# RWKV-6 attention, Fourier mixing and an MLP on one core: twelve chunks instead of six transposed by DMA, and a new written-out order

## The chip, the cores and the metric

The kernel runs on 1 core of one Trainium2 chip. The metric is device microseconds of one launch, and lower is better. In short below: PE is TensorE, DVE is VectorE, ACT is ScalarE, POOL is GpSimd, SP is SyncE.

## The reference, cut to what matters

Batch 4, 8 heads, 768 time steps, head dimension 48, all in fp32. First a recurrent attention:

```python
for t in range(S):
    cur = einsum('bhd,bhe->bhde', u * k[t], v[t])
    y[t] = einsum('bhd,bhde->bhe', r[t], state + cur)
    state = w[t][..., None] * state + einsum('bhd,bhe->bhde', k[t], v[t])
```

Its result is laid out as x of (4, 768, 384) and goes through a mixing layer:

```python
u = x + real(fft(fft(x, axis=1), axis=2))
un = (u - mean(u)) / sqrt(var(u) + 1e-6)
out = u + maximum(un @ w_ch1, 0) @ w_ch2      # 384 -> 1536 -> 384
```

## The kernel before

**Attention.** A batch is cut into 6 chunks of 128 time steps, so there are 24 chunks, numbered n = 6b + c; "chunk 2.3" is chunk 3 of batch 2. `attention(b, c)` (line 923) takes one chunk: ACT takes the logarithm of w (`lb`), PE sums it along the chunk with two triangular matrices (lines 939 and 943), ACT takes the exponentials (lines 945 and 958), and the result scales r (line 977, on DVE, in `rkh`) and k (through the helper at line 532, on POOL or DVE, in the other half of `rkh`). Both are then turned, so that the head dimension lies on the partitions: `rkh` (time by head and dimension) becomes `rkt`. From `rkt` PE forms the scores (line 1009, 8 matmuls), DVE masks them (line 1014), and PE forms the output from the masked scores and v (line 1059) and from the carried state (line 1056). The six chunks of batch 0 are done in pairs by `attention2`, with work of the same kind.

**The turning** is done in one of two ways, chosen by `n >= DMA_T`. Below it, PE transposes r and k in 4 matmuls each (lines 993 and 999) into two PSUM banks, and ACT or DVE copies each bank to `rkt` (lines 555 and 556, a tile of 128x512). From it on, one transposing DMA on SP's queue (line 985) turns both at once, from SBUF to SBUF. `DMA_T` is 18: the six chunks of batch 3 go by DMA, those of batches 1 and 2 by PE. The activations of the MLP (`un`, line 1169 on PE, line 1175 as a DMA) are turned the same two ways; with `DMA_U = 2`, batches 2 and 3 go by DMA.

**Mixing and MLP.** `mix(b)` takes the Fourier transforms as matmuls with tables (lines 1123 and 1146), normalizes, and runs the MLP on two halves of 384 rows: 72 matmuls of 128x384 with w_ch1 (line 1193), the ReLU on ACT or DVE (lines 1200 and 1198), 72 with w_ch2 (line 1211), the last sum on DVE (line 1215) and a store (line 1219).

**Data.** The inputs come in as 128x8x48 pieces of 192 KB, one DMA for each of w, k, r and v of a chunk (line 592; batch 0 in pairs, line 584). All loads, stores and transposing DMAs but the two for the MLP's weights stand in one queue, SP's, and SP takes them one after another: where it waits for data to transpose, the loads behind it wait too. Each input has 7 buffers; `rkh` and `rkt` have 4.

**Order.** Nothing is left to run time. The kernel records all its operations, and the table `ORDER` says for each of the five engines in which order it runs them and, where an operation may run on several engines, on which. The table came from a planner, outside the kernel, that works with the lengths in the code (an operation's second argument, and `xfer`, `DMA_SET`, `T_RK` and their like for DMAs). The kernel runs that plan once while it is built (`schedule`), only to give tiles their PSUM banks and to place the waits; the lengths have no effect on the chip beyond that.

Of the kernel before, what the change touches and what calls it, by code (L numbers as in the profile page):

```python
# [22 lines left out]
DMA_T, DMA_U, T_RK, T_UN, T_XFER = 18, 2, 1750, 2000, 1800  # L23
# [35 lines left out]
    "act": (  # L59
# [12 lines left out]
    "dve": (  # L72
# [15 lines left out]
    "pool": (  # L88
# [11 lines left out]
}  # L100


class _Tile:


# [26 lines left out]
class _Prog:  # L132
# [7 lines left out]
    DMA_SET, DMA_POST, DMA_SW = 1400, 300, 2000  # L140
# [1147 lines left out]
```

## Time and profile before

| | us |
|---|---|
| three runs | 184.34, 185.72, 187.69 |
| median | 185.72 |
| the profiled execution, its own time | 186.0 |
| its span, first to last instruction | 184.2 |
| PE busy in the span | 175.2 (95%) |
| DVE, ACT, POOL busy | 155.6, 123.4, 105.0 |
| share of the 16 DMA engines, SP's queue | 63.8% |

The span is divided by the profile in several views: busy time by stretch, the chain of work that ended last (each piece with what released it), groups of instructions by source line, and waits by engine. A matmul's duration there is the time from its start to its modelled end; matmuls overlap, so the pace of a run of them is read from the chain, where only the part that moves the chain on is counted. A DMA's row has the time that SP needed to issue it; "to landing" is from issue to the last byte.

### The profile page before, as it was taken

The page shows a single profiled execution, that of the slowest core. Times are in us where ns is not written, and L with a number is a line of the kernel's source. Part 1 is how long each engine was busy: PE and PEld are TensorE (multiplying, and loading weights), DVE is VectorE, ACT ScalarE, POOL GpSimd, SP SyncE. Part 2 cuts the span into 40 slices and gives each one's busy share as a digit, 9 for nine tenths or more (in the row PEclk, how much of TensorE's full clock was granted, in tenths as well). Part 3 has the DMA queues.
Part 4 walks back from the last instruction along what each step waited for, and adds up shares of the span by engine and source line. Part 5 has one row for each costly group of instructions (what it writes and reads, how often), then busy time and mean ns, then how long its engine had stood idle before and what let it go on. Part 6 is the DMA issues. An engine that isn't in the chain of part 4 may idle for free.

```text
span 184.2 us, 4725 instructions
## 1 busy us (share of the span) xinstructions
PE 175.2 (95%) x1824; PEld 125.8 (68%) x1824; DVE 155.6 (84%) x374; ACT 123.4 (67%) x291; POOL 105.0 (57%) x126
## 2 busy tenths in 40 slices
PE   5989999999999999899997999999999999999993
PEld 2446677776778777577865777668787766887661
DVE  8999999999989999989999789999797497551343
ACT  4898999998999676699986789836514521146010
POOL 2027998699785739999796386994654330000000
PEclk9999999999999999999999999999999999999999
DMA  5999899999999998998989996635601014520033
GB/s 154 320 324 256 189 180 178 182 196 214 149 204 194 184 192 170 210 264 165 194 211 206 204 205 171 117 66 114 191 4 43 4 43 109 130 102 4 0 126 130
DMA packets 102599, 29.00 MB, mean 157 GB/s; under 512 B 98865, under 2 KB 102066, under 8 KB 102450
## 3 DMA queue, kind: packets, MB, share of 16 engines
q1 hardware_dynamic: 102034, 26.36, 63.8%
q0 software_dynamic: 544, 2.36, 7.0%
q8 instruction: 14, 0.23, 0.5%
q14 instruction: 7, 0.06, 0.1%
HBM read 23.59 MB, written 4.72 MB: 154 GB/s over the span
## 4 chain that ended last, share of the span: by engine, by line
PE 53%; DVE 16%; ACT 11%; POOL 6%; SPq 5%; DMA 4%; issue 3%; POOLq 0%; DVEq 0%
PE bank L1211 20%; PE bank L1193 16%; SPq L592 5%; PE bank L1146 4%; ACT rkt L555 2%; PE bank L1123 2%; DMA in_v<-in_v_dram 2%; PE bank L1232 2%; DMA in_w<-in_w_dram 2%; DVE x L1065 2%; DVE rkh L532 2%; POOL rk L532 2%; ACT lb L546 1%; DVE ah L1014 1%; ACT vb L546 1%
## 5 line engine op out<-in xcount | busy, mean ns | idle before, releaser
L1193 PE MATMUL bank<-unt,w 128*128 128x384 bf16 x288 | 55.6, 328 | 0.1
L1211 PE MATMUL bank<-w,ht 128*128 128x384 bf16 (+2 forms) x300 | 54.8, 320 | 0.0
L1200 ACT ACTIVATE ht<-bank 128x384 bf16<-128x384 f32 x72 | 32.9, 497 | 24.5 <-PE bank L1193 24.2
L1193 PEld LDWEIGHTS bank<-unt,w 128*128 128x128 bf16 x288 | 38.8, 144 | 6.2 <-ACT ht L1200 0.4
L1211 PEld LDWEIGHTS bank<-w,ht 128*128 128x128 bf16 x300 | 28.1, 98 | 15.2
L1014 DVE TENSOR_TENSOR ah<-bank,msk 128x512 bf16<-128x512 f32 x36 | 23.1, 680 | 1.0 <-PE bank L1009 1.0
L532 POOL TENSOR_TENSOR rk<-rk,ub 128x384 f32<-128x384 f32 x21 | 21.0, 1006 | 2.8 <-DVE rk L532 2.0
L1215 DVE SCALAR_TENSOR_TENSOR osb<-bank,rstd,uf 128x384 f32<-128x384 f32 (+2 forms) x25 | 14.8, 593 | 6.6 <-ACT rstd L1183 3.8
L532 POOL TENSOR_TENSOR vtd<-in_v,dc 128x384 f32<-128x384 f32 (+1 forms) x23 | 19.1, 834 | 2.2 <-DVE dc L966 1.1
L1198 DVE TENSOR_SCALAR ht<-bank 128x384 bf16<-128x384 f32 x24 | 12.5, 550 | 8.9 <-PE bank L1193 8.9
L555 ACT ACTIVATE rkt<-bank 128x512 bf16<-128x512 bf16 x28 | 17.2, 637 | 1.7 <-PE bank L999 0.7
L532 POOL TENSOR_TENSOR rk<-in_r,in_k 128x384 f32<-128x384 f32 x17 | 17.1, 1014 | 1.9 <-DMA in_k<-in_k_dram 0.9
L532 POOL TENSOR_TENSOR rkh<-in_k,e 128x384 bf16<-128x384 f32 x16 | 15.9, 1004 | 2.9 <-ACT e L958 1.7
L532 POOL TENSOR_TENSOR xf<-sd 128x382 bf16<-128x382 f32 (+1 forms) x12 | 12.0, 1003 | 8.1 <-DVE sd L532 3.1
L532 POOL TENSOR_TENSOR sd<-x 128x385 f32<-128x385 f32 x8 | 8.1, 1007 | 10.7 <-DVE sd L532 8.8
L546 ACT ACTIVATE un<-uf,agg 128x384 bf16<-128x384 f32 x18 | 10.8, 620 | 3.9 <-DVE agg L1154 3.9
L1148 DVE TENSOR_TENSOR uf<-bank,x 128x384 f32<-128x384 f32 x24 | 12.5, 546 | 0.6 <-PE bank L1146 0.5
L1152 DVE BATCH_NORM_STATS2 bst<-uf 128x6 f32<-128x384 f32 x24 | 12.9, 547 | 0.1
L546 ACT ACTIVATE lb<-in_w 128x384 bf16<-128x384 f32 (+1 forms) x21 | 11.8, 572 | 1.5 <-DMA in_w<-in_w_dram 1.4
L546 ACT ACTIVATE vb<-in_v 128x384 bf16<-128x384 f32 x23 | 11.8, 520 | 1.2 <-DMA in_v<-in_v_dram 1.2
L977 DVE TENSOR_TENSOR rkh<-bank,in_r 128x384 bf16<-128x384 f32 x18 | 9.8, 549 | 2.5 <-ACT bank L945 1.5
L945 ACT ACTIVATE bank<-bank 128x384 f32<-128x384 f32 x18 | 8.8, 488 | 3.9 <-PE bank L939 3.9
(163 smaller groups left out, 359.7 us busy)
## 6 DMA issues: line engine op xcount, KB each, us to landing
out_dram<-osb SPq DMA_DIRECT2D x23, 192.0 KB, 2.1
in_w<-in_w_dram SPq DMA_DIRECT2D x18, 192.0 KB, 4.0
in_r<-in_r_dram SPq DMA_DIRECT2D x18, 192.0 KB, 4.4
in_k<-in_k_dram SPq DMA_DIRECT2D x18, 192.0 KB, 4.2
in_v<-in_v_dram SPq DMA_DIRECT2D x18, 192.0 KB, 4.1
w<-in_moe_w_ch_dram POOLq DMA_DIRECT2D x2, 1152.0 KB, 9.6
in_r<-in_r_dram SPq DMA_DIRECT2D x3, 384.0 KB, 4.6
in_k<-in_k_dram SPq DMA_DIRECT2D x3, 384.0 KB, 4.2
```

The lines of the kernel that those rows point to most:

```text
L532: return lambda e: e.tensor_tensor(out=o, in0=a, in1=b, op=f)
L546: return lambda e: e.activation(o, a, f, **kw)
L555: {"act": lambda e: e.activation(o(), i(), ACTF.Copy), "dve": lambda e: e.tensor_copy(out=o(), in_=i())}, **kw)
L977: op("dve", v_1(DM), lambda e: e.tensor_tensor(out=rh[:, :, 0:D], in0=ps(tce)[:, 0:DM].rearrange("t (h d) -> t h d", d=D), in1=rt[:, :, :] ...
L1014: masked[n] = op("dve", v_1(512), lambda e, x=x: e.tensor_tensor(out=ah[:, x:H:2, :], in0=ps(ta[x])[:, :].rearrange("p (h t) -> p h t", t= ...
L1148: op("dve", v_1(DM), lambda e, kb=kb, t=t: e.tensor_tensor(out=uf[:, kb, :], in0=ps(t)[:, 0:DM], in1=xb[:, kb, 0:DM], op=ALU.add), r=[t, ( ...
L1152: op("dve", v_1(DM), lambda e, kb=kb, bs=bs: e.bn_stats(bs[:, :], uf[:, kb, :]), r=[("UF", i, kb)], w=[("BST", n % 4)])
L1193: ins = e.matmul(ps(t)[:, 0:384], W1[:, m, j:HID:NJ], unt[:, :, m, :], start=(m == 0), stop=(m == NM - 1))
L1198: {"dve": lambda e, j=j, t=t, ht=ht: e.tensor_scalar(out=ht[:, j, :], in0=ps(t)[:, 0:384], scalar1=-1.0, scalar2=0.0, op0=ALU.mult, op1=AL ...
L1200: "act": lambda e, j=j, t=t, ht=ht: e.activation(ht[:, j, :], ps(t)[:, 0:384], ACTF.Relu, scale=-1.0)},
L1211: ins = e.matmul(ps(t)[:, 0:hi - lo], ht[:, j, 128 * x:128 * x + 128], W2[:, j, lo:hi], start=(j == 0), stop=(j == NJ - 1))
L1215: op("dve", v_1(hi - lo) + 64, lambda e, kb=kb, t=t, o=o, lo=lo, hi=hi: e.scalar_tensor_tensor(out=o[:, lo:hi], in0=ps(t)[:, 0:hi - lo], s ...
```

## The change

`DMA_T` goes from 18 to 12: the chunks of batch 2 are also turned by transposing DMAs (12 in all, of 128x8x128), and the 48 matmuls and 12 copies that turned them are gone. The lengths that the planner works with are set anew: transposes 1800 to 1400 (r and k) and 1580 (`un`), single loads 960 to 1040, double loads 1350 to 1320 and 1240, stores 520 to 670, the start of a DMA 1400 to 1200; double loads may not start in the plan before 700. `ORDER` is made anew for all engines. Nothing else is changed: 7 input buffers, 4 buffers of `rkh` and `rkt`, the same matmuls elsewhere.

```diff
-DMA_T, DMA_U, T_RK, T_UN, T_XFER = 18, 2, 1750, 2000, 1800
+DMA_T, DMA_U, T_RK, T_UN, T_XRK, T_XUN = 12, 2, 1750, 2000, 1400, 1580
...
 ORDER = {
     "pe": (
-        "6 1437 1438 1439 1440 1441 1442 1443 1444 86 92 1445 94 1446 ...
+        "6 1419 1420 1421 1422 1423 1424 1425 86 1426 92 1427 1428 94 ...
...
-    DMA_SET, DMA_POST, DMA_SW = 1400, 300, 2000
+    DMA_SET, DMA_POST, DMA_SW = 1200, 300, 2000
...
-               w=[("in", n, i), ("in", n, i + 1)], sem="in_%s%d" % (n, i), xfer=1350)
+               w=[("in", n, i), ("in", n, i + 1)], sem="in_%s%d" % (n, i), xfer=1240 if c else 1320)
+        o.ready0 = 700
...
-               w=[("in", n, i)], sem="in_%s%d" % (n, i), xfer=960)
+               w=[("in", n, i)], sem="in_%s%d" % (n, i), xfer=1040)
...
-               r=[("RH", i4), ("KH", i4)], w=[("RTB", i4), ("KTB", i4)], sem="rkt%d" % i4, xfer=T_XFER)
+               r=[("RH", i4), ("KH", i4)], w=[("RTB", i4), ("KTB", i4)], sem="rkt%d" % i4, xfer=T_XRK)
...
-                   sem="unt%d" % ((2 * b + hf) % 2), xfer=T_XFER)
+                   sem="unt%d" % ((2 * b + hf) % 2), xfer=T_XUN)
...
-                       r=[("OSB", n % 3, lo)], w=[("out", b, kb, lo)], sem="out%d" % (n % 3), xfer=520)
+                       r=[("OSB", n % 3, lo)], w=[("out", b, kb, lo)], sem="out%d" % (n % 3), xfer=670)
```

Line numbers of the changed kernel are higher by 2 in most of the code (line 993 is 995 there, 1009 is 1011, 985 is 987).

What the new order moves is shown at three places. The first is PE's program at chunks 2.2 and 2.3. Before, with `bank<-idw,rkh` the transposes, `bank<-rkt` the scores (8 for each chunk) and `bank<-w,ht` the MLP:

```order
L999 MATMUL bank<-idw,rkh 128x128 x4
L1035 MATMUL bank<-vb,rkh 128x96 x4
L1211 MATMUL bank<-w,ht 128x384 x4
L993 MATMUL bank<-idw,rkh 128x128 x8
L1211 MATMUL bank<-w,ht 128x384 x8
L1009 MATMUL bank<-rkt 128x128 x16
```

Now, at the scores of chunks 2.1 and 2.2, with `bank<-idw,un` the transposes that stay on PE, those of the MLP of batch 1:

```order
L1171 MATMUL bank<-idw,un 128x128 x3
L1213 MATMUL bank<-w,ht 128x384 x4
L951 MATMUL bank<-pb,idw 128x8
L954 MATMUL bank<-one,lb 128x2 x4
L1011 MATMUL bank<-rkt 128x128 x16
L1213 MATMUL bank<-w,ht 128x384 x8
```

The transposes of r and k are gone ahead of the scores; what PE waits for there is now a landing of SP's queue.

The second is SP's queue where the loads of batch 2 give way to those of batch 3. Before, there is no transposing DMA until row 67 of SP's program, six loads before the end of the loads; a piece of it from the loads of batch 2:

```order
L592 DMA in_w<-in_w_dram 128x8x48
L592 DMA in_r<-in_r_dram 128x8x48
L592 DMA in_k<-in_k_dram 128x8x48 x2
L592 DMA in_r<-in_r_dram 128x8x48
L592 DMA in_k<-in_k_dram 128x8x48
L592 DMA in_r<-in_r_dram 128x8x48
L592 DMA in_v<-in_v_dram 128x8x48 x2
```

Now, from the first transposing DMA on, those of chunks 2.0, 2.1 and 2.2:

```order
L987 DMA_TRANSPOSE rkt<-rkh 128x8x128
L594 DMA in_r<-in_r_dram 128x8x48
L594 DMA in_w<-in_w_dram 128x8x48
L594 DMA in_v<-in_v_dram 128x8x48
L594 DMA in_r<-in_r_dram 128x8x48
L594 DMA in_w<-in_w_dram 128x8x48 x2
L1221 DMA out_dram<-osb 128x384
L987 DMA_TRANSPOSE rkt<-rkh 128x8x128
L594 DMA in_k<-in_k_dram 128x8x48
L987 DMA_TRANSPOSE rkt<-rkh 128x8x128
```

Loads now stand behind transposes that wait for DVE and POOL. Up to the last load of r, SP's program has 10 transposes of r and k and one of `un`, where it had 2 and none.

The third is PE's program at the last scores, those of chunks 3.4 and 3.5. Before:

```order
L1193 MATMUL bank<-unt,w 128x384 x15
L1211 MATMUL bank<-w,ht 128x384 x4
L1009 MATMUL bank<-rkt 128x128 x16
L1211 MATMUL bank<-w,ht 128x384 x4
L1193 MATMUL bank<-unt,w 128x384 x3
```

Now:

```order
L1195 MATMUL bank<-unt,w 128x384 x9
L1037 MATMUL bank<-vb,rkh 128x96 x4
L1213 MATMUL bank<-w,ht 128x384 x4
L1011 MATMUL bank<-rkt 128x128 x16
L1213 MATMUL bank<-w,ht 128x384 x4
L1195 MATMUL bank<-unt,w 128x384 x6
```

The rows read alike; the place differs. Before, 120 MLP matmuls of line 1193 and 140 of 128x384 of line 1211 stand behind these scores, now 96 and 112. Over the whole program the new order also moves some work between engines: ACT has 78 ReLUs (72 before) and DVE 18 (24 before), and the very first DMA of SP's queue is now the load of w for chunk 1.0, ahead of those for the first pair of chunks.

121 rows, old and new, of the table ORDER are left out of this document.

## The prediction

> **What bounds the kernel now.** I read the busy times by stretch first, then PE's own waits, then the chain that ended last. By stretch (columns: length, then busy us and instructions of each engine, the granted clock, the share of the 16 DMA engines, GB/s):
>
> ```profile
> 0.00:10.00 10.00, 7.52 (x25) 3.03 (x25) 8.62 (x53) 6.85 (x12) 1.38 (x9) 1.00 0.89 244
> 10.00:20.00 10.00, 9.11 (x127) 5.63 (x127) 10.00 (x25) 9.44 (x19) 6.28 (x9) 1.00 1.06 262
> 20.00:30.00 10.00, 9.84 (x237) 7.37 (x235) 10.00 (x22) 10.00 (x24) 10.00 (x14) 1.00 0.96 196
> ...
> 70.00:80.00 10.00, 9.46 (x115) 6.98 (x115) 9.02 (x19) 7.46 (x17) 9.57 (x11) 1.00 0.99 219
> 80.00:90.00 10.00, 10.00 (x121) 7.38 (x119) 10.00 (x24) 9.72 (x25) 9.48 (x11) 1.00 0.94 183
> 90.00:100.00 10.00, 9.89 (x106) 7.35 (x104) 10.00 (x22) 7.63 (x20) 8.47 (x9) 1.00 0.97 208
> 100.00:110.00 10.00, 9.00 (x83) 6.64 (x83) 8.14 (x17) 8.10 (x21) 4.72 (x7) 1.00 0.99 202
> 110.00:120.00 10.00, 10.00 (x98) 7.01 (x95) 9.80 (x24) 8.73 (x23) 8.30 (x10) 1.00 0.66 147
> ```
>
> Two things are full at once up to 110 us: PE (the first busy number; 9.00 to 10.00 of every 10 from 20 us on) and the DMA engines (0.94 to 1.06 in the stretches shown). Which of them sets the end? PE's own waits after the first 30 us:
>
> ```profile
> PE bank L1169 <- ACT un L546: 1.2, 2, 1.0
> PE bank L943 <- ACT lb L546: 0.5, 1, 0.5
> PE bank L939 <- DVE x L1065: 0.3, 1, 0.3
> ```
>
> That is all, 2.0 us in 154. None names a load or the tile `rkt`, although batch 3 is already turned by DMA. The chain agrees (start, us that it moved on, what):
>
> ```profile
> 73.37 3.67 DMA in_w<-in_w_dram
> ...
> 80.37 0.45 PE bank L993 x8
> ...
> 96.20 3.75 DMA in_v<-in_v_dram
> ...
> 101.55 0.65 PE bank L1211 x4
> ...
> 129.99 0.55 PE bank L1009 x16
> ...
> 160.00 6.83 PE bank L1193 x42
> ...
> 175.12 5.23 PE bank L1211 x40
> 180.45 0.60 DVE osb L1215
> 181.10 0.62 DVE osb L1215
> ```
>
> It runs over a load twice, last at 96 to 100 us, and from 101.55 us to 180.35 us over matmuls alone. So PE's amount of work sets the end, and DMA is a full second resource that PE's cover hides.
>
> **The change, part by part.** *Removed on PE:* the eight transposes of one chunk move the chain on by 0.45 us, 56 ns each. Six chunks have 48, so 48 x 0.056 = **2.7 us**. The other side of that price is the group of the 24 for k in the transposing stretch, where overlapping tails count as busy:
>
> ```profile
> L555 ACT ACTIVATE rkt<-bank 128x512 bf16<-128x512 bf16 x9 | 5.2, 599 | 0.7 <-PE bank L999 0.7
> ...
> L977 DVE TENSOR_TENSOR rkh<-bank,in_r 128x384 bf16<-128x384 f32 x6 | 3.3, 548 | 1.0 <-DMA in_r<-in_r_dram 1.0
> ...
> L993 PE MATMUL bank<-idw,rkh 128*128 128x128 bf16 x24 | 2.0, 219 | 0.0
> ...
> L556 DVE COPY rkt<-bank 128x512 bf16<-128x512 bf16 x3 | 1.3, 417 | 0.2 <-PE bank L999 0.2
> ```
>
> 2.0 us for 24 is 83 ns each, or 4.0 us for 48. I take 2.7, since the chain counts only what PE's next instruction waits for; the range keeps 2.7 to 4.0.
>
> *Removed on ACT and DVE:* 12 copies, 9 x 0.599 + 3 x 0.417 = 6.6 us. They lie beside PE's work (PE waited for neither in the rows above, but for 1.2 + 0.5 us of ACT's), and the new order puts six more ReLUs on ACT. I count nothing; at most it is worth those 1.7 us.
>
> *Added on the DMA engines:* six transposes. What one holds is read where two ran with nothing behind them, and how long it takes from its own line:
>
> ```profile
> 115.00:119.00 4.00, 4.00 (x50) 2.71 (x49) 4.00 (x12) 3.13 (x9) 4.00 (x6) 1.00 0.70 135
> ...
> L985 SPq DMA_TRANSPOSE rkt<-rkh x6: 1231/1254/1804, 101.0 to 126.0; - x6
> ...
> DMA to landing us min/median/max: 3.0/3.2/3.9
> ...
> L592 SPq DMA_DIRECT2D in_r<-in_r_dram x18: 464/996/2242, 14.0 to 110.5; - x18
> ...
> DMA to landing us min/median/max: 3.4/4.1/11.3
> ```
>
> 0.70 x 4.00 us / 2 = 1.4 us of all 16 engines each. In a queue that is full to 110 us this delays what stands behind it, one for one. Before the last load of r stand 8 more transposes of r and k and one of `un` than before (10 and 1 against 2 and 0), so it is issued about 9 x 1.4 = 12.6 us later, at 110.5 + 12.6 = 123.1 us, and lands 4.1 us later, at 127.2. Then follow DVE's scaling of r (line 977, 0.55 us) and the transpose itself, 3.2 to 3.9 us: `rkt` of the last chunk is there at 131.7 us.
>
> When is it wanted? The last scores started at 129.99 us. In the new order 52 more MLP matmuls (24 + 28) of 6.83 / 42 = 163 ns stand ahead of them, 8.5 us, and 2.7 us of transposes do not: due at 129.99 + 8.5 - 2.7 = 135.8 us. The new order gives PE other work for as long as the data is late, with 4.1 us to spare. So the 12.6 us cost nothing, unless that reserve is used up; what then comes late are the last scores and all that stands behind them in PE's fixed order, one for one.
>
> *A longer way for each chunk of batch 2.* From `rkh` to `rkt` it was eight transposes and a copy, 0.45 + 0.60 = 1.05 us; now it is 3.2 to 3.9 us, so 2.2 to 2.9 us later, six times. If the order covers none of it that is 6 x 2.9 = 17 us, if it covers all, nothing. The nearest rows are the six transposes of batch 3, the same way in the same kernel, on which PE has no wait: I take 0 and keep up to 0.5 us for each chunk (3 us) in the range. Queued behind a transpose that waits are SP's loads; the waits of that line today are:
>
> ```profile
> SPq L985 <- POOL rkh L532: 4.4, 2, 4.1
> SPq L985 <- DVE osb L1215: 1.8, 1, 1.8
> SPq L985 <- DVE sd L532: 1.6, 1, 1.6
> SPq L985 <- DVE dc L966: 1.3, 1, 1.3
> ```
>
> 9.1 us for six, 1.5 us each. With a load landing 4.1 us after its issue and an issue about every 1.0 us, some four loads are under way at any time, so a wait of 1.5 us at SP leaves the DMA engines with work.
>
> *The new first load.* The load of w for chunk 1.0 now goes ahead of w for the first chunks, which ACT's logarithm reads:
>
> ```profile
> L584 SPq DMA_DIRECT2D in_w<-in_w_dram x3: 1150/1151/1202, 1.8 to 7.9; - x3
> ...
> DMA to landing us min/median/max: 3.6/4.8/5.8
> ...
> 6.41 1.28 ACT L702 ACT_TABLE_LOAD   x1
> 7.78 0.84 ACT L546 ACTIVATE lb<-in_w 128x768 bf16<-128x768 f32 x1
> ```
>
> That w is issued at 1.8 us and landed by about 6.6; ACT is busy with a table until 7.69. One more load ahead costs about 1.0 us, so 7.6: still hidden, at worst 1.2 us on a start that DVE and ACT limit. Taken as 0.
>
> *The rest of the order:* the same matmuls in another sequence. PE's idle time is 2.48 + 0.89 + 0.16 us in the first three stretches and 0.54 + 0.00 + 0.11 + 1.00 + 0.00 in the five later ones that are shown. All of it is what a better or worse order can win; a worse one has no such bound. I take 0.
>
> **Sum:** 186.0 us (the profiled execution's own time: a span of 184.2 and 1.8 around it) - 2.7 = 183.3. That execution is 0.3 us above the median of the three runs, 185.7, so I predict **183.0 us** for the median.
>
> **Rivals.**
>
> *Given back on the way to the scores.* The 2.2 to 2.9 us per chunk are not fully covered: with 0.45 us open in each of six chunks the 2.7 us are gone and the time is 185.7. For it: the transposes of batch 2 run beside full DMA engines (0.94 to 0.99 from 70 to 110 us), those of batch 3 mostly not. Against it: two of batch 3 were issued among the loads, from 101.0 us, and nothing on PE waited for them by name, though 100 to 110 us is also PE's emptiest stretch (9.00).
>
> *Also fewer waits.* The order rests on loads and transposes nearer to what the rows show, and ACT and DVE lose 6.6 us. If PE's waits on ACT (1.7 us) and a little of the loss at the start go as well, 183.0 - 2.0 = 181.0. For it: 1.00 us of PE idle in 100 to 110 us, just behind the load that the chain ran over. Against it: orders that fit one pace exactly have no reserve when another run is slower.
>
> *The DMA queue runs dry, and the last batch comes late.* SP waits at ten transposes before the last load of r. If each leaves the DMA engines idle for today's mean of 1.5 us, the last `rkt` lands 15 us later, at 146.7: 10.9 us after it is due, and 183.0 + 10.9 = 194. The point from which it decides is 4.1 us of idle DMA in all; at 11 us the time is 190. For it: the longest of those waits was 4.1 us, as long as the queue's reserve. Against it: the mean is 1.5, and SP's order has three to seven other transfers between most of the transposes.
>
> *A PE transpose is worth its whole duration.* The row of 24 has a mean of 219 ns; 48 x 0.219 = 10.5 us, so 175.2. Against it: eight of them move the chain by 0.45 us, so they overlap. The Trainium skill's page "TensorE: Matmul & The Clock Gate", section "Part 4: PE-mode transpose", gives about 275 ns for one inside a kernel; by that the sum would be 185.7 - 13.2 = 172.5, an estimate from the page, and the trace disagrees with 56 ns. Another page speaks against the whole change: the Trainium skill's "VectorE: DVE Perf Modes", section "Rules for kernel authors", says to transpose 128x128 on TensorE where the result may go to PSUM and by DMA otherwise, and its section "The three transpose paths" has 1309 ns for one block by DMA, so 10.5 us for a chunk's eight, as an estimate. The trace disagrees here too: all eight land in 3.2 us.
>
> **How the numbers follow.** The forecast (-2.7 us; 181.7 with 4.0 off instead, 184.5 with half of the 3 us) has 0.45, given back (184.5 to 188.0) 0.24, fewer waits (180.5 to 182.0) 0.17, the dry queue (188 and more) 0.12, the whole duration 0.02. The range of **180.5 to 188.0 us** holds the first three. Two per cent, about what a measurement of this kernel can tell from no change, is 182.0 and 189.4. Faster by more than that are the last case, fewer waits and some of the forecast's lower edge: 0.25. Slower is most of the dry queue: 0.10. Within: 0.65.
>
> **What would show it.** Right: 48 matmuls fewer on PE; no wait of PE on `rkt` or `rkh` over 0.5 us in a chunk; the last load of r issued near 123 us; the last scores near 136 us; from about 105 us to the end a chain of matmuls alone; the whole 2 to 3 us shorter. Wrong: a DMA share that falls below 0.9 in any stretch from 60 to 110 us with SP waiting at the transposes means the dry queue; waits of PE ahead of the scores of batch 2 (line 1011 there) mean the gain was given back; more than 0.5 us of added PE idle in the first 20 us means that the new first load was not free; a chain that runs over DMA after 110 us means that PE's amount of work no longer sets the end.

## The result and the profile after

| | kernel before | changed kernel |
|---|---|---|
| median of the comparison, us | 185.78 | 184.04 (182.36 to 188.22) |
| ratio, 95% interval | 1 | 0.990 [0.987, 0.993] |
| forecast | | 183.0, range 180.5 to 188.0 |

The changed kernel is 1% faster, clear of the noise and within the 2% that count as no change. It was run again beside each set of experiments and then took 184.22, 183.01 and 182.27 us where the kernel before took 184.48, 184.34 and 184.38: ratios of 0.9956 [0.992, 0.999], 0.9898 [0.986, 0.993] and 0.9901 [0.987, 0.993]. A time in us is the median of all executions, while a ratio and its interval leave out the long ones, so that a ratio can lie lower than the two medians beside it say. The profile shown here is that of the second repeat (182.86 us, span 180.8, PE at full clock throughout).

The page's first part, before and then after, gives each engine's busy us and its instructions:

```profile
span 184.2 us, 4725 instructions
PE 175.2 (95%) x1824; PEld 125.8 (68%) x1824; DVE 155.6 (84%) x374; ACT 123.4 (67%) x291; POOL 105.0 (57%) x126
```

```profile
span 180.8 us, 4648 instructions
PE 172.5 (95%) x1776; PEld 123.9 (69%) x1776; DVE 153.1 (85%) x366; ACT 124.0 (69%) x292; POOL 98.3 (54%) x121
```

PE has 48 matmuls fewer and 175.2 - 172.5 = 2.7 us less to do. The stretch from 60 to 70 us before, which the prediction left out, and then the stretches after the change, in the columns of the prediction's first view:

```profile
60.00:70.00 10.00, 10.00 (x114) 7.17 (x108) 9.78 (x21) 6.57 (x18) 5.99 (x7) 1.00 0.95 185
```

```profile
0.00:10.00 10.00, 7.81 (x26) 3.12 (x27) 8.99 (x50) 6.93 (x12) 1.98 (x14) 1.00 0.88 231
10.00:20.00 10.00, 9.09 (x129) 5.71 (x130) 9.38 (x25) 9.42 (x21) 6.87 (x8) 1.00 1.10 288
...
60.00:70.00 10.00, 10.00 (x111) 7.25 (x110) 9.99 (x22) 6.62 (x18) 4.80 (x6) 1.00 0.83 160
70.00:80.00 10.00, 10.00 (x96) 6.69 (x95) 9.77 (x25) 7.17 (x17) 4.14 (x6) 1.00 1.14 211
80.00:90.00 10.00, 10.00 (x101) 7.73 (x96) 9.60 (x22) 7.95 (x18) 9.61 (x11) 1.00 0.90 191
90.00:100.00 10.00, 9.10 (x107) 7.01 (x106) 8.82 (x19) 7.36 (x20) 8.78 (x10) 1.00 0.92 182
100.00:110.00 10.00, 10.00 (x101) 7.33 (x100) 8.70 (x18) 6.32 (x17) 4.41 (x5) 1.00 0.90 192
110.00:120.00 10.00, 10.00 (x90) 6.26 (x88) 9.82 (x23) 5.18 (x12) 5.91 (x7) 1.00 0.95 189
120.00:130.00 10.00, 9.10 (x90) 7.00 (x88) 8.74 (x20) 7.84 (x21) 8.11 (x9) 1.00 1.14 188
```

Two things are to be seen. After the start, PE's emptiest stretches are now 90 to 100 and 120 to 130 us (9.10 each). And the DMA share, 0.94 to 0.99 from 60 to 110 us before, now swings between 0.83 and 1.14 there; its mean over these five stretches is 0.94, where it was 0.97, so the queue ran dry in places and not throughout. PE's waits after the first 30 us, then pieces of the chain that are no matmuls, up to the one that it waits for at 129.68 us:

```profile
PE bank L945 <- ACT ht L1202: 0.9, 1, 0.9
PE bank L1011 <- DMA rkt<-rkh: 0.9, 1, 0.9
```

```profile
93.19 4.99 DMA rkt<-rkh
...
112.91 0.94 DVE bst L1154 x2
117.46 1.85 DVE ah L1016 x3
122.96 1.04 DVE osb L1217 x2
125.02 3.31 DMA in_w<-in_w_dram
128.35 0.52 ACT lb L547
...
129.68 0.34 PE bank L945
```

PE has two waits of 0.9 us. One is for a transposing DMA by name, that of chunk 2.5. The other is put down to ACT, but the chain shows what ACT had waited for: the load of w of chunk 3.5, which stands behind the transposing DMA of chunk 3.3 in SP's queue and was issued at 125.02 us. Before the change the chain left the DMAs for good at 100 us. SP's waits at the transposing DMAs (the four longest rows; five shorter ones make it 17.6 us at twelve DMAs, 1.5 each as before):

```profile
SPq L987 <- DVE sd L533: 3.5, 1, 3.5
SPq L987 <- POOL rk L533: 3.5, 3, 2.8
SPq L987 <- DVE agg L1156: 2.9, 1, 2.9
SPq L987 <- DVE xf L533: 2.6, 1, 2.6
```

The queue itself, by lines of issue and landing and by the scores (line 1011; first and last start are the two times behind the durations):

```profile
L987 SPq DMA_TRANSPOSE rkt<-rkh x12: 1233/1297/3319, 65.0 to 132.3; - x12
...
DMA to landing us min/median/max: 3.1/3.4/5.4
```

```profile
L594 SPq DMA_DIRECT2D in_r<-in_r_dram x18: 464/822/5652, 15.6 to 126.3; - x18
...
L1011 PE MATMUL bank<-rkt x144: 212/216/227, 32.7 to 135.8; 48*128 48x128 bf16 x144
```

The last load of r is issued at 126.3 us, the last transpose at 132.3; that lands 3.1 us later at the earliest, at 135.4, and the last of its scores starts at 135.8. Nothing waits there, but next to nothing is in hand either.

### The profile page after: what moved, and what is told of

Its sections match the earlier page's. It is cut to its first block, busy times and chain, and to the rows that moved or that the text cites. A ratio compares the mean times of both kernels' runs of the same rounds, so it can differ in the third digit from the quotient of the medians.

```text
span 186.2 us, 4648 instructions
## 1 busy us (share of the span) xinstructions
PE 175.1 (94%) x1776; PEld 125.4 (67%) x1776; DVE 152.9 (82%) x366; ACT 124.5 (67%) x292; POOL 98.4 (53%) x121
## 4 chain that ended last, share of the span: by engine, by line
PE 53%; DVE 18%; DMA 14%; SPq 7%; ACT 3%; issue 2%; POOL 2%; DVEq 0%
PE bank L1213 18%; PE bank L1195 17%; DMA in_k<-in_k_dram 6%; DMA in_w<-in_w_dram 5%; PE bank L1125 4%; PE bank L1148 3%; DVE ah L1016 3%; SPq L585 3%; SPq L594 3%; DMA rkt<-rkh 3%; PE bank L1011 2%; DVE x L1067 2%; DVE osb L1217 1%; DVE uf L1150 1%; DVE bst L1154 1%
## 5 line engine op out<-in xcount | busy, mean ns | idle before, releaser
L1195 PE MATMUL bank<-unt,w 128*128 128x384 bf16 x288 | 54.0, 328 | 0.0
L1213 PE MATMUL bank<-w,ht 128*128 128x384 bf16 (+2 forms) x300 | 53.6, 320 | 0.0
L1202 ACT ACTIVATE ht<-bank 128x384 bf16<-128x384 f32 x78 | 35.5, 495 | 15.5 <-PE bank L1195 14.9
L533 POOL TENSOR_TENSOR rk<-rk,ub 128x384 f32<-128x384 f32 x22 | 21.9, 1005 | 11.6 <-DVE rk L533 6.6
L533 POOL TENSOR_TENSOR rkh<-in_k,e 128x384 bf16<-128x384 f32 x21 | 21.1, 1005 | 10.4 <-DVE one L544 4.9
L547 ACT ACTIVATE un<-uf,agg 128x384 bf16<-128x384 f32 x20 | 12.2, 624 | 10.2 <-DVE agg L1156 10.1
L533 POOL TENSOR_TENSOR rk<-in_r,in_k 128x384 f32<-128x384 f32 x15 | 15.3, 1021 | 3.7 <-DMA in_k<-in_k_dram 3.7
L556 ACT ACTIVATE rkt<-bank 128x512 bf16<-128x512 bf16 x20 | 12.2, 640 | 0.0
L1067 DVE TENSOR_TENSOR x<-bank,vtd 128x384 f32<-128x384 f32 x18 | 9.7, 548 | 1.7 <-PE bank L1061 1.7
L1200 DVE TENSOR_SCALAR ht<-bank 128x384 bf16<-128x384 f32 x18 | 9.6, 549 | 1.4 <-PE bank L1195 1.4
L960 ACT ACTIVATE e<-bank 128x392 f32<-128x392 f32 (+1 forms) x18 | 8.9, 497 | 1.8 <-PE bank L954 1.7
```

The costliest lines, as they stand in the source:

```text
L533: return lambda e: e.tensor_tensor(out=o, in0=a, in1=b, op=f)
L547: return lambda e: e.activation(o, a, f, **kw)
L556: {"act": lambda e: e.activation(o(), i(), ACTF.Copy), "dve": lambda e: e.tensor_copy(out=o(), in_=i())}, **kw)
L1067: op("dve", v_1(DM), lambda e: e.tensor_tensor(out=xb[:, c, 0:DM], in0=ps(ty)[:, 0:DM], in1=vtd[:, :, :].rearrange("t h d -> t (h d)"), op ...
L1195: ins = e.matmul(ps(t)[:, 0:384], W1[:, m, j:HID:NJ], unt[:, :, m, :], start=(m == 0), stop=(m == NM - 1))
L1202: "act": lambda e, j=j, t=t, ht=ht: e.activation(ht[:, j, :], ps(t)[:, 0:384], ACTF.Relu, scale=-1.0)},
```

## The experiments

Theory at the outset: PE's amount of work sets the end; the 48 transposes are worth their 2.7 us, and the new order covers the longer way of the DMA. Rivals: the gain is the new order's alone; PE has slack anyhow; the DMA queue is the limit.

**The changed kernel again** (three times, no edit).

> The changed kernel once more, for a profile at an undisturbed clock. Theory (48 transposes less on PE, some of it given back): 1.5 to 2.7 us below the kernel before; PE's idle time after 30 us at most 1 us above the 2.2 us of before; the last load of r issued 10 to 20 us later than 110.5 us; from about 105 us to the end a chain of matmuls. Rival (the new first load costs the start): 0.5 us or more of added PE idle in the first 20 us.

> The changed kernel, unaltered, beside the next three. Both theories: 0.990 to 0.996 of the kernel before, PE busy about 173 us, a hole on PE of about 1.4 us at 32 to 34 us that ends with the k of chunk 1.0 (in some executions none).

> The changed kernel, unaltered, beside the next three: 0.990 to 0.996 of the kernel before; four or five of twelve executions with a mean granted clock of 0.98 or 0.99 and 2 to 3 us longer than the others.

Measured: the three ratios above. The first fell short of its 1.5 to 2.7 us: it is 0.8 us (0.1 to 1.5) below the kernel before. The other two lie at the lower edge of what was expected. In the third, two executions of twelve had a mean granted clock of 0.991, not four or five. The hole at 32 to 34 us was in the first of these profiles only; it is taken up below.

**The new order without the DMAs.**

```diff
-DMA_T, ..., T_XUN = 12, ..., 1580
+DMA_T, ..., T_XUN = 18, ..., 1580
 ORDER (of the changed kernel)
-  sp: the six transposing DMAs of batch 2
+  pe: 48 transposes of batch 2, at most 3 us ahead of their scores; act, dve: 9 and 3 copies behind them
```

> The new order, with batch 2 turned by PE again: its six transposing DMAs are taken from SP's order, and its 48 matmuls and 12 copies (9 on ACT, 3 on DVE) put in at most 3 us ahead of each chunk's scores. Theory (the gain is PE's 2.7 us): 2.0 to 3.5 us slower than the changed kernel, so 0 to 1.5 us above the kernel before. Rival (the gain is the new order's, made with better lengths, and the transposing DMAs bring nothing): within 0.7 us of the changed kernel.

Measured: 186.66 us, 1.0118 [1.007, 1.017] of the kernel before, so (1.0118 - 0.9956) x 184.5 = 3.0 us more than the changed kernel beside it. PE:

```profile
PE 174.8 (95%) x1824; PEld 126.2 (68%) x1824; DVE 154.5 (84%) x369; ACT 128.4 (70%) x301; POOL 98.4 (53%) x121
```

174.8 - 172.5 = 2.3 us of the 3.0 are PE's work. The 3.0 lie in the 2.0 to 3.5 that were expected, but the place against the kernel before does not: 1.2% or 2.2 us above it, and not 0 to 1.5. This order without the DMAs loses against the old one, so the gain is not this order's alone. Where the transposes stand in it was set for this run and not planned. An order planned anew, with the new lengths, for six transposing DMAs was not tried, so that a part of the gain may still be the planner's.

**The DMAs in the old order.**

```diff
 (kernel before)
-DMA_T, ... = 18, ...
+DMA_T, ... = 12, ...
 ORDER (of the kernel before)
-  pe, act, dve: transposes and copies of batch 2
+  sp: six transposing DMAs, each where its r and k are scaled
```

> The old order, with only the way of turning batch 2 changed: the matmuls and copies are taken out and each transposing DMA put into SP's queue where its data is ready. Theory (the way by DMA is 2.2 to 2.9 us longer and must be covered by the order, which here it is not; from rkh to the scores the old order has 2.3 to 6.5 us): 0 to 4 us slower than the kernel before, with waits of PE on rkt. Rival (PE's amount of work alone decides): 2.0 to 2.7 us faster than before.

Measured: 196.08 us, 1.0612 [1.056, 1.066], 11.3 us more than before: far outside what was expected. PE's longest wait, two pieces of the chain, and three stretches:

```profile
PE bank L1012 <- DMA rkt<-rkh: 7.5, 2, 4.0
```

```profile
72.58 3.73 DMA rkt<-rkh
86.26 4.13 DMA rkt<-rkh
```

```profile
70.00:80.00 10.00, 5.96 (x48) 3.68 (x47) 4.45 (x9) 2.95 (x6) 6.18 (x7) 0.80 1.03 209
80.00:90.00 10.00, 7.09 (x59) 4.09 (x57) 6.78 (x17) 5.74 (x14) 7.56 (x9) 0.84 0.75 155
90.00:100.00 10.00, 9.48 (x81) 6.19 (x82) 6.75 (x13) 4.72 (x13) 4.63 (x6) 0.68 0.75 147
```

Two waits of about 4 us on the turned r and k leave PE idle for 4.04 + 2.91 + 0.52 us, and the granted clock (third number from the end) is down to 0.80, 0.84 and 0.68 in the same stretches: if the array ran at half clock for the missing share, that is (0.20 + 0.16 + 0.32) x 20 = 13.6 us at half clock, which lengthens the matmuls in it by up to 6.8 us. By this estimate 7.5 us of waits and 6.8 of clock, less the 2.7 of the transposes, are 11.6 us, near the 11.3 measured. The expectation counted the waits and left out the clock. In the old order, with each DMA put where its data is ready, the swap does not pay.

**PE's work put back, nothing else.**

```diff
 def amat(e):
+    if b == 2:
+        for i in range(8):
+            e.transpose(psb(ta[i // 4])[:, 128 * (i % 4):128 * (i % 4) + 128], IDB[:, :], IDB[:, :])
     for q in range(HP):
```

Eight needless transposes of the identity stand ahead of each chunk's scores in batch 2; the scores overwrite them.

> The changed kernel, with PE doing 48 transposes of the same size (of the identity, into the banks that the scores then overwrite) ahead of the scores of batch 2, and no copies. The output is the same. Theory (PE's work sets the end, 56 ns each): 2.2 to 3.2 us slower than the changed kernel. Rival (PE has slack there, and the gain came from ACT and DVE losing 12 copies): at most 0.7 us slower. Rival (a transpose costs its whole 219 ns): 10 us slower.

Measured: 186.11 us, 1.0034 [0.999, 1.008]: 0.0078 x 184.5 = 1.4 us more than the changed kernel beside it, on 174.6 - 172.5 = 2.1 us more work of PE. That is between the theory (2.2 to 3.2) and the rival (up to 0.7), and the two intervals leave 0.4 to 2.5 open: PE's work counts, and some of it may fall into time in which PE would have waited.

**Six more transfers on SP's queue.**

```diff
 if n >= DMA_T:
     op("sp", T_RK, lambda e: e.dma_start_transpose(...), ...)
+    if b == 2:
+        op("sp", 750, lambda e: e.dma_start(out[3, chunk c], w[3, :, chunk c]), ..., sem="dup")
```

> The changed kernel with one more transfer on SP's queue behind each of the six transposing DMAs of batch 2: 192 KB from the input w to the rows of the output that are written at the end (a needless copy that is overwritten later), as long on the DMA engines as a load at least (about 1.0 us each, 6 us in all). Theory as the trace of the changed kernel now reads (no reserve left: the last transposed r and k landed at 136.9 us, 0.1 us ahead of their scores at 137.0): 4 to 8 us more than the changed kernel. Rival (the reserve of 4.1 us as predicted): 0 to 2 us more. Rival (DMA fully hidden): nothing.

Measured: 189.22 us, 1.0172 [1.010, 1.025], (1.0172 - 0.9898) x 184.3 = 5.0 us more than the changed kernel beside it. That is what was expected of a kernel without a reserve, 4 to 8 us. The last load of r is issued at 132.2 us, 5.9 us later than above:

```profile
L596 SPq DMA_DIRECT2D in_r<-in_r_dram x18: 434/764/4906, 16.1 to 132.2; - x18
```

But the 5.0 us (3.5 to 6.6 by the two intervals) were not lost at the last scores, whose reserve was in question. PE's two emptiest stretches after the start and its two longest waits:

```profile
90.00:100.00 10.00, 7.83 (x83) 6.09 (x81) 9.29 (x20) 5.07 (x14) 9.67 (x11) 1.00 1.08 200
100.00:110.00 10.00, 7.84 (x91) 5.65 (x92) 5.31 (x11) 4.80 (x14) 4.51 (x5) 1.00 0.98 214
```

```profile
PE bank L947 <- ACT lb L549: 2.3, 1, 2.3
PE bank L1127 <- ACT xf L1101: 2.0, 1, 2.0
```

From 70 to 110 us PE is idle for 5.7 us, where the changed kernel has 0.9; from 110 to 150 us it is idle for 0.05. Behind both waits stands ACT, which waited 3.7 and 2.6 us for loads of w that were issued right behind a needless transfer, at 95.8 and 100.8 us. So the expected time came, by another way than the expectation had: the late loads of w cost it, some 30 us ahead of the last scores, and this run does not say how much was in hand there. It does show that the DMA engines are a second limit beside PE in this stretch, and not a covered one.

**Loads of batch 1 earlier.** The first repeat had shown PE idle at 32.4 to 33.9 us:

```profile
33.16 0.56 DVE L533 TENSOR_TENSOR rkh<-in_k,e 128x384 bf16<-128x384 f32 x1 [1.83 <-DMA in_k<-in_k_dram]
...
33.86 0.59 PE L1001 MATMUL bank<-idw,rkh 128*128 128x128 bf16 x4 [1.44 <-ACT xf L1083]
```

PE's own wait is put down to ACT, but DVE, which makes what PE turns there, waited for k of chunk 1.0. In the new order that load stands three places too late. Two kernels move loads, a third moves work of PE as well:

```diff
 sp: ... w1.3
+k1.0
 v1.2 v1.1 w1.4
-k1.0
 k1.2 ...
```

> The changed kernel with one load moved: k of chunk 1.0 three places earlier in SP's order, ahead of v of chunks 1.2 and 1.1 and w of chunk 1.4 (these had 4 to 5 us to spare). Theory (part of the 2.7 us was lost to that late load): PE's wait at 32 to 34 us (1.4 us) goes, and with it the low granted clock behind it (0.83 in 30 to 40 us); 1.4 to 2.8 us less than the changed kernel. Rival (the loads and transposes later on set the pace, so that time won at 30 us is lost again at the transpose of chunk 2.5 or at the last scores): under 0.5 us less, with a wait of PE on rkt at 95 to 101 us longer by what was won.

```diff
 (as above, and)
 pe:
+  two groups of four matmuls with w_ch2 (line 1213)
   scores of chunk 2.5
-  the two groups, behind the next one
```

> As the kernel before this one (k of chunk 1.0 earlier), and on PE two groups of four MLP matmuls of the second layer (1.3 us) moved from behind the scores of chunk 2.5 to ahead of them. Theory (PE's amount of work sets the end, and its two holes are the loss): the wait of 0.9 us on the transposed r and k of chunk 2.5 goes too; 0.7 to 1.0 us less than with the load alone. Rival (the scores of chunk 2.5 are themselves on the way to the end): no gain, since their 1.3 us later start is passed on.

```diff
 sp: ... w1.3
+k1.0
 v1.2 v1.1 w1.4
-k1.0
+w1.5 r1.3
 k1.2 r1.2 k1.3
-r1.3 w1.5
 v1.3 ...
```

> The changed kernel with three loads of batch 1 earlier in SP's order: k of chunk 1.0 three places earlier, and w of chunk 1.5 and r of chunk 1.3 ahead of k of chunk 1.2, so that all three are under way well before the 1.15 MB load of weights from POOL's queue, behind which a load took 10 us to land. Theory (those loads make the hole on PE at 32 to 46 us and the low clock behind it, in some executions): at most one execution in ten with a mean clock below 0.995, median at 182.0 to 182.8 us where the kernel before takes 184.3. Rival (the low clock has another source): as many such executions as the unaltered kernel, same median.

Measured: 183.15, 183.87 and 182.42 us, 0.9903 [0.986, 0.994], 0.9890 [0.983, 0.995] and 0.9899 [0.986, 0.994], where the unaltered kernel beside them had 0.9898, 0.9898 and 0.9901. No gain is seen in any. Low clocks did not get rarer either: 6 of 13, 3 of 6 and 2 of 6 executions had a mean below 0.995, the unaltered kernel 4 of 12 and 2 of 12 beside them. So the theories of the first and the third fell. In the second, PE's wait on the transpose of 2.5 went from 0.9 to 0.2 us, but other waits came in its place: from 90 to 110 us PE is idle for 0.92 us where it was 0.90. That hole is passed on, as its rival said; the intervals alone are too wide to exclude 0.7 us.

Why the first and third gained nothing is in part open. The profile at full clock of the unaltered kernel has no hole at 32 us, so there is nothing to gain in such an execution. The profiled executions of the two kernels had mean clocks of 0.973 and 0.982, and show that the hole came back at another load. Their chains run over w of 1.5 and k of 1.3:

```profile
33.76 10.02 DMA in_w<-in_w_dram
```

```profile
33.97 11.04 DMA in_k<-in_k_dram
```

Both were issued just ahead of a load on another queue, here in the first of the two:

```profile
33.76 0.83 SPq L596 DMA_DIRECT2D in_w<-in_w_dram  x1
...
34.03 0.98 POOL L754 DMA_DIRECT2D w<-in_moe_w_ch_dram  x1
```

Other loads of w land 3.6 us after their issue (the median of the profile above); these loads took 10 and 11 us. The one was issued 0.27 us, the other 0.55 us ahead of POOL's 1.15 MB load of weights, which goes out when POOL comes to it and not in SP's order. That POOL's load held them up is read from these two executions, and was not tested; if it did, moving one load ahead only makes another one the last before it. Tying POOL's load to a place in SP's queue was not tried.

**Loads ahead of the transposes that wait.**

```diff
 (as the last one, and)
 sp:
+r2.2 w2.3
 transpose of 2.0
-r2.2 w2.3
+v2.4
 transpose of 2.3
-v2.4
+w3.1
 transpose of 2.5
-w3.1
+k3.1 k3.2
 transpose of 3.0
-k3.1 k3.2
+w3.5
 transpose of 3.3
-w3.5
```

> As the kernel before this one, and seven more loads ahead of the transposing DMA behind which they stood on SP's queue while it waited for its scaled r and k: r of 2.2 and w of 2.3 ahead of the transpose of 2.0, v of 2.4 ahead of that of 2.3, w of 3.1 ahead of 2.5, k of 3.1 and 3.2 ahead of 3.0, w of 3.5 ahead of 3.3. Theory (SP's waits at the transposes leave the DMA engines idle for about 4 us and hold up the loads of w on the way to the scores): 0.5 to 2 us less than with the batch 1 loads alone, and a DMA share nearer to 1 in 60 to 70 and 100 to 110 us. Rival (PE's amount of work sets the end and these waits are covered): less than 0.3 us either way. Rival (the transposes now queue behind the loads and come late for their scores): 0.5 us or more slower.

Measured: 181.17 us (180.72 to 183.33), 0.9847 [0.980, 0.990] of the kernel before, and 1.1 us less than the 182.27 of the changed kernel beside it; four of its six executions are shorter than the shortest of the other's twelve (181.52), though the two intervals still touch. Two stretches and the last load of r:

```profile
60.00:70.00 10.00, 10.00 (x108) 7.17 (x105) 9.98 (x22) 6.80 (x18) 4.71 (x6) 1.00 1.02 188
...
100.00:110.00 10.00, 9.90 (x99) 6.97 (x97) 9.49 (x19) 7.14 (x19) 5.23 (x6) 1.00 0.95 202
```

```profile
L596 SPq DMA_DIRECT2D in_r<-in_r_dram x18: 448/759/3278, 15.6 to 124.1; - x18
```

The DMA share is 1.02 where it was 0.83 and 0.95 where it was 0.90, though at 80 to 90 us it is 0.80 where it was 0.90. The last load of r goes out 2.2 us earlier, and behind 8 us the chain runs over no DMA any more. Both of PE's waits of 0.9 us are gone, that for the transposed r and k of chunk 2.5 and that behind w of chunk 3.5, one of the loads that were moved. So what stood behind the waiting transposes was on the way to the end. This version is clearly faster than the kernel before and the fastest here. Against the kernel with only the loads of batch 1 moved (182.42 us) it wins 1.2 us, within the 0.5 to 2 that were expected.

**Holes on PE.**

```diff
 op("pe", ..., f, r=[...] + ["W1"]
+   + ([("MK2", hf)] if b == 3 and j == 5 else []), w=[t] + ([("MK", hf)] if b == 3 and (hf, j) in ((0, 3), (1, 0)) else []))
+op("pool", 1000, multiply of 192 columns (hf 0), of 384 and of 192 columns (hf 1), r=[("MK", hf)], w=[("MK2", hf)])
```

> The changed kernel with two holes made on PE in the last stretch, where it does matmuls alone: a matmul of batch 3 waits for a needless multiply on POOL that itself waits for the matmul before it (the product goes to an input buffer that is read no more). One multiply of 192 columns near 157 us (hole of about 0.9 us), two of 384 and 192 columns near 169 us (about 1.9 us). Theory (a longer hole lowers the granted clock behind it): clock 1.00 after the short hole, about 0.5 for some 3 us after the long one, so 4.0 to 5.0 us more than the changed kernel at full clock. Rival (the clock falls for another reason and PE then waits): 1.00 after both, 2.8 us more.

Measured: 185.50 us, 1.0085 [1.005, 1.012], (1.0085 - 0.9901) x 184.4 = 3.4 us more than the changed kernel beside it. PE waited for the needless multiplies and the clock did not move (the two stretches hold one hole each):

```profile
PE bank L1197 <- POOL in_w L1200: 2.6, 2, 1.8
```

```profile
155.00:158.00 3.00, 2.20 (x14) 1.68 (x13) 1.08 (x4) 0.97 (x2) 0.59 (x1) 1.00 0.47 123
168.00:172.00 4.00, 2.20 (x15) 1.56 (x13) 1.54 (x3) 0.00 (x0) 1.58 (x2) 1.00 0.13 49
```

The holes of 0.8 and 1.8 us cost 3.4 us (2.5 to 4.3), which does not tell the rival's 2.8 from the theory's 4.0; the clock does. The theory that a hole of more than some 1.5 us lowers the clock each time fell.

## Why the prediction was right, and where not

The time was right: 184.04 us against 183.0, inside the range, and in the direction that was forecast. But three of the prediction's own signs of being wrong came as well: a DMA share below 0.9 with SP waiting at the transposes (0.83), a wait of PE over 0.5 us ahead of scores of batch 2 (0.9), and a chain over a DMA after 110 us. Step by step:

*The 48 transposes at 56 ns.* Right: PE's busy time fell by 2.7 us, just the sum. Of it 1.4 us (0.4 to 2.5) showed when the work was put back alone, and 0.8 to 1.9 us by the ratios of the four comparisons. The two waits below, 1.8 us, are where the rest can have gone; the kernel that has neither is 1.1 us faster.

*The copies and the first load at nothing.* No run showed a price. PE is busy for 7.81 + 9.09 us in the first two stretches and was for 7.52 + 9.11. The copies were not put back on their own.

*The last scores due at 135.8 us.* Near: their group begins at 135.5 us in the chain, where it began at 129.99, and its last matmul at 135.8. A part of that is luck. In the kernel with the loads moved ahead PE's program is the same and the last of these matmuls starts at 133.7 us, 2.1 earlier; the sum carried along the waits of the old order (PE is idle for 5.8 us up to 130 us there), and the new one happened to have about as many (5.2 us).

*A reserve of 4.1 us there.* This is the step that failed. The last load of r went out at 126.3 us, not 123.1. The last transposing DMA was issued 6.0 us behind it, where the sum had 4.7, and landed at about 135.4 us, not 131.7. So at most some 0.4 us were in hand. That "a wait of 1.5 us at SP leaves the DMA engines with work" did not hold everywhere: the waits were 1.5 us on average as foreseen, but the share fell to 0.83, and with loads moved ahead of the waiting transposes the last load of r went out at 124.1. The forecast of 123.1 also counted only what was added. Two loads of v that stood ahead of the last load of r now stand behind it, and one more store ahead of it, so by its own pace of about 1.0 us for a load it should have been some 1 us earlier.

What the late queue cost was not at the last scores, where PE waited for nothing, but at two places on the way: 0.9 us for the transposed r and k of chunk 2.5 and 0.9 us behind w of chunk 3.5. The prediction asked when r and the transposes come; it left out the loads of w, which stand behind the same transposes. So the rival "the DMA queue runs dry" was right in its mechanism for a part of the queue, and far off in its price: the last transposed r and k landed 3.7 us later than forecast, and not 15.

*Matmuls alone from about 105 us.* Wrong for the same reason: the chain ran over DVE at 111 to 124 us and over the load of w at 125. By the test that the prediction named, a chain over DMA after 110 us, PE's amount of work no longer set the end there.

*The longer way from `rkh` to `rkt` at nothing.* Nearly right with the new order: one wait of 0.9 us in twelve transposes. It was worth nothing that could be measured when it was removed alone. With the old order it cost 11.3 us net of the transposes saved; the prediction had 17 for the case that nothing covers it.

*A transpose worth its whole duration* (10.5 us) fell with the 2.7 us of busy time.

## What to carry to other kernels

What a unit of work on the busiest engine is worth is read from the pace of a run of them, here 56 ns and not 219, and it is won only as far as the order lets it: the same swap cost 11.3 us in the old order and won 1 to 2 in a new one. When work goes to a queue that is taken in order, look at all that stands behind it, and not only at the transfers whose amount changes: here loads of w stood behind waiting transposes, and seven loads moved ahead of five such waits gave 1.1 us more. A margin that is the difference of two long sums (131.7 and 135.8 us here) is no margin until a run has shown it. A few needless transfers are a cheap test of a queue, but read in the trace where their time went: here it was lost some 30 us ahead of the margin that they were meant to test.

## What the hardware showed beside this

*The granted clock halves for about 3.4 us at a time.* The first repeat of the changed kernel, around its hole at 32.4 us:

```profile
30.00:32.00 2.00, 2.00 (x53) 1.54 (x50) 1.33 (x3) 2.00 (x6) 1.32 (x2) 1.00 1.00 198
32.00:34.00 2.00, 0.56 (x10) 0.32 (x7) 0.84 (x3) 2.00 (x6) 0.00 (x0) 0.95 0.57 108
34.00:36.00 2.00, 2.00 (x19) 1.27 (x18) 2.00 (x6) 1.56 (x4) 0.60 (x2) 0.50 1.07 211
36.00:38.00 2.00, 2.00 (x18) 1.06 (x17) 1.37 (x4) 0.77 (x2) 1.54 (x2) 0.70 0.99 192
```

At 0.50 for half clock, the four rows hold (0.05 + 0.50 + 0.30) x 4 = 3.4 us of it. In the third repeat a wait of 0.8 us at 8.4 us was followed by as much (clocks of 0.86, 0.50 and 0.79 in 8 to 14 us). In the kernel with the DMAs in the old order it was 13.6 us, four times that. The Trainium skill's page "TensorE: Matmul & The Clock Gate", section "Part 1: The HAM clock gate (the "warmup" mystery)", has a free-running window of 3413 ns over which the clock is decided and a half-rate state after an idle window; the traces agree with that length. They do not agree with an idle window as its condition: a hole of 1.4 us was followed by half clock at 32 us, and one of 1.8 us in the last stretch was not. That it depends on where a hole falls in the window would fit both; no run here shows it, and it stays open.

Of 54 executions of the changed kernel 17 had a mean granted clock of 0.991 or less, and 3 of 69 of the kernel before beside the repeats. Most of the 17 took 1 to 3 us longer than the others; one took 188.22 us, and one, with a mean clock of 0.659, took 250.27 us and has no profile. Why the changed kernel meets the low clock more often was not tested. None of the six executions with the loads moved ahead had it, but two of six of the kernel with only the loads of batch 1 moved did, and SP's order is the same in both up to about 60 us, ahead of which it fell in every profiled execution that had it in the new order: six executions do not tell these two apart.
